# The last sum of the output done on VectorE instead of by accumulating DMAs, and layer one's last second products dealt among layer two's first products

## The chip, the cores and the metric

The kernel runs on one core of a Trainium2 chip. Time is device time in microseconds (us) of one execution; smaller is better. Engines: PE (TensorE matmul, with its weight loads PEld), DVE (VectorE), ACT (ScalarE), POOL (GpSimd), SP (SyncE, which here only issues DMAs).

## What is computed

Attention for 2 batches of 8 heads (768 tokens, head width 64) in which a query sees only the keys of its own hash bucket, then two dense layers over the 1536 tokens:

```python
attn_out = _attn_ref(**attn_kwargs)                       # masked softmax attention, f32
x = attn_out.transpose(0, 2, 1, 3).reshape(B * S, H * D)  # (1536, 512)
h = x @ w_in                                              # layer one, 512 -> 2048
g = h - np.tanh(h)
x = g @ w_out                                             # 2048 -> 512
g = x @ w_gate                                            # layer two, 512 -> 1536
silu = g * (1.0 / (1.0 + np.exp(-g)))
val = x @ w_val
out = silu * val @ w_out2                                 # 1536 -> 512
```

The weights come as 64-bit floats and are converted on the chip. Each f32 operand is split into a high and a low part, and a product is three matmul passes (high x high, high x low, low x high).

## The kernel before, in words

**Halves and blocks.** The 1536 tokens are two halves `sb` of 768 (one for each batch), and each half is two blocks `t` of 384. The hidden width is cut into chunks `i` of 256 columns: 8 for layer one, 6 for layer two.

**First products.** For a chunk and a half, `products` makes `x @ w` by Strassen's scheme: seven products `m` = 0 to 6 of six matmuls each (128x384), from seven sums of blocks of `x` (A11, S1, A12, S2, S4, S3, A22), which `x_blocks` makes ahead: ACT copies the high part (L361), DVE or POOL subtracts it for the low part (L363), and further sums come from DVE or POOL (L368). One such set of seven is a "unit". Layer one has 16 units `in`; layer two has 24, `gate` and `val` for each chunk and half. ACT and DVE take the products out of PSUM (L830, L833), form tanh or silu, and split the result for the second product (L779, L784).

**Second products.** `out_group` is one group of six matmuls into one PSUM bank (a ring of four banks). Layer one has 8 groups for each chunk and half (128x384), layer two has 6 (128x512; three, `m` = 0 to 2, for each block `t`). A group's sum is copied from PSUM by ACT or DVE (L923) to a staging slot in SBUF. When the groups of a block are staged, one DMA on POOL's queue adds the slot to what is there already: in SBUF for layer one (L931), in DRAM, to the output itself, for layer two (L940, 768 KB; the first chunk is a plain store on SP's queue, L938). Layer one's last chunk is added by DVE (L917), because the next layer's `x_blocks` reads the sum; each half's `x_blocks` is declared behind the half's last group.

**The order.** The program first lists all operations in a nominal order, with `clock` counting PE's time, and gives each a due time. `Plan.order` then plays the list: each engine takes the ready operation that is due first, with the costs written in the list; those of the second part (all behind `n_first`) are multiplied by `SAFE` except on PE. The order that it finds for each engine is the program; on the chip each engine's queue runs in that order, waiting at semaphores. The nominal order interleaves neighbouring units, and deals the second products among the first products by a `credit` for each first product: 8/7 of a group while `n` (the unit's number) is below 20, 3/7 after. When the unit that ends layer one is finished, `flush` puts out all that is left of its groups at once. What is left when the products are over follows behind them.

**Staging slots.** Layer two's four slots lie where layer one's sums were (`stage`, L749). The four (half, block) pairs take them in turn, so a chunk uses the slot that the same pair had a chunk earlier.

Of the kernel before, what the change touches and what calls it, by code (L numbers as in the profile page):

```python
# [14 lines left out]
ALU = mybir.AluOpType  # L15
# [3 lines left out]
NB, NH, S, D = 2, 8, 768, 64  # L19
NBITS = 6  # L20
NPAIR = NH // 2
TB = 384
NTK = NB * S
NSB = NTK // S
DM = 512
KT = DM // 128
F1, F2 = 2048, 1536
NP1, NP2 = F1 // 256, F2 // 256
# [36 lines left out]
class Plan:  # L65
# [4 lines left out]


    LAT = 0.14
    SAFE = 1.1

    def __init__(self):
        self.ops = []
# [3 lines left out]
    def op(self, eng, fn, r=(), w=(), due=0.0, lat=None, late=False, after=0.0, alt=None, port=()):  # L80
        n = len(self.ops)
        deps = set()
        for k in r:
            deps.update(self.writers.get(k, ()))
        for k in w:
            deps.update(self.writers.get(k, ()))
            deps.update(self.readers.get(k, ()))
        for k in r:
            self.readers.setdefault(k, []).append(n)
        for k in w:  # L90
            if k in r:
                self.writers.setdefault(k, []).append(n)
            else:
                self.writers[k] = [n]
                self.readers[k] = []
        deps.discard(n)
        eng = {e: t * (1 if e == "PE" or not self.n_first else self.SAFE) for e, t in eng.items()}
        self.ops.append((eng, fn, deps, due, self.LAT if lat is None else lat, late, after,
                         DUE["alt"] if alt is None else alt, port))
# [86 lines left out]
def lsh_attention_moe_kernel(ctx: ExitStack, tc: tile.TileContext, qT, kT, vP, proj, cst, wts, out):  # L186
# [3 lines left out]
    op = plan.op  # L190
# [48 lines left out]
    def ring(name, n):  # L239

        c = counts[name] = counts.get(name, -1) + 1
        return name, c % n
# [12 lines left out]
    def dve(n):  # L255
        return (n + 151) / 960 - 0.01
# [78 lines left out]
    def need(key, due, after=0.0):  # L335
        while key not in wkey:
            k = stream.pop(0)
            (declare_out if k[0].startswith("out") else declare_in)(*k, due, after)
        return wkey[key]
# [409 lines left out]
    def stage(layer, m):  # L749

        if m == 0:
            stages[layer] = ring(("st", layer), (2, 4)[layer - 1])[1]
        r = stages[layer]
        key = "st", layer, r, m
        size = (TB, DM)[layer - 1]
        first = []
        if key not in used:
            used.add(key)
            if layer == 1:
                first = [("xf", r, m)]  # L760
            else:
                first = [("acc", r // 2, 4 * (r % 2) + k) for k in range(m * DM // TB, ((m + 1) * DM - 1) // TB + 1)]
        if layer == 1:
            at_ = lambda n=1: ct_a[:, (8 + 4 * r + m) * TB:(8 + 4 * r + m + n) * TB]
        else:
            at_ = lambda n=1: late["acc"][r // 2][:, (r % 2) * 1536 + m * DM:(r % 2) * 1536 + (m + n) * DM]
        return at_, key, first

    stages = {}
# [3 lines left out]
        return op_t[i], k, w  # L773

    ALT = 2.0
    EARLY, XDUE, EALT, ZDUE = 14, 13, 1.0, (0, 10)

    def tt(dst, dk, a, ak, b, bk, alu, due, port):
        op({"DVE": dve(TB), "POOL": pool(TB)} if port else {"DVE": 0.56}, lambda e: e.tensor_tensor(out=dst, in0=a, in1=b, op=alu),  # L779
# [35 lines left out]
    def bank_slot():  # L815
        return RING[ring("bank", len(RING))[1]]
# [62 lines left out]
    def acc_at(sb, j, n=1):  # L879
        return late["acc"][sb][:, j * TB:(j + n) * TB]  # L880

    def out_group(layer, i, sb, j):
        d = clock[0]
        dur = 6 * (MM3, MM5)[layer - 1]
        clock[0] += dur
        name = ("out", "out2")[layer - 1]
        wks = [need((name, 2 * i + f), d) for f in range(2)]
        n = (4, 3)[layer - 1]
        t, m = divmod(j, n)
        size = (TB, DM)[layer - 1]  # L890
        gs = [gh[layer, i, sb, t, f] for f in range(2)]
        k, ps = bank_slot()
        ps = ps[:, 0:size]

        def mm(e):
            c = 0
            for f in range(2):
                w = wo_t[wks[f][1]]
                for wpart, gpart in terms:
                    if layer == 1:  # L900
                        lhs, rhs = w[:, wpart, m * 128:m * 128 + 128], gs[f][gpart]
                    else:
                        lhs, rhs = gs[f][gpart][:, m * 128:m * 128 + 128], w[:, wpart, :]
                    e.matmul(out=ps, lhsT=lhs, rhs=rhs, start=c == 0, stop=c == 5)  # L904
                    c += 1

        op({"PE": dur}, mm, r=[wk + (h,) for wk in wks for h in range(2)] + [g for gg in gs for g in gg[2]], w=[k],
           due=d, lat=0.25)
        e = clock[0]
        aks = [("acc", sb, n * t + c) for c in range(n)]  # L910
        if layer == 1 and i in (0, NP1 - 1):
            if i == 0:
                op({"DVE": dve(TB), "ACT": 0.5}, lambda g:
                   g.activation(out=acc_at(sb, j), in_=ps, func=ACTF.Copy) if g is nc.scalar else
                   g.tensor_copy(acc_at(sb, j), ps), r=[k], w=[("acc", sb, j)], due=e, late=True)
            else:
                op({"DVE": 0.57}, lambda g: g.tensor_tensor(  # L917
                    out=acc_at(sb, j), in0=ps, in1=acc_at(sb, j), op=ALU.add,
                ), r=[k, ("acc", sb, j)], w=[("acc", sb, j)], due=e, late=True)
        else:  # L920
            at_, key, first = stage(layer, m)
            op({"ACT": 0.18 + size / 1200, "DVE": dve(size)}, lambda g, at_=at_:
               g.activation(out=at_(), in_=ps, func=ACTF.Copy) if g is nc.scalar else g.tensor_copy(at_(), ps),  # L923
               r=[k], w=[key] + first, due=e, late=layer == 2, alt=EALT)
            if m == 0:
                stages[layer, "at"] = at_
            if m == n - 1:
                at_ = stages[layer, "at"]
                keys = [key[:3] + (c,) for c in range(n)]
                if layer == 1:  # L930
                    op({"POOL": 1.0}, lambda g, at_=at_: g.dma_start(out=acc_at(sb, 4 * t, 4), in_=at_(4), accum_op=ALU.add),  # L931
                       r=keys + aks, w=aks, due=e + 1, lat=5.0, late=True)
                else:
                    o = out[sb * S + t * TB:sb * S + t * TB + TB, :].rearrange("(j p) c -> p j c", p=128)
                    src = lambda at_: at_(3).rearrange("p (j c) -> p j c", j=3)
                    ok = ("o", sb, t)
                    if i == 0:
                        op({"SP": 0.5}, lambda g, at_=at_: g.dma_start(out=o, in_=src(at_)), r=keys, w=[ok], due=e + 1, lat=4.0)  # L938
                    else:
                        op({"POOL": 1.0}, lambda g, at_=at_: g.dma_start(out=o, in_=src(at_), accum_op=ALU.add),  # L940
                           r=keys + [ok], w=[ok], due=e + 1, lat=5.0)
        if layer == 1 and i == NP1 - 1 and j == 7:
            x_blocks(sb, [0, 1], lambda name, ks: acc_at(sb, ACC[name] + ks[0], len(ks)), lambda name, k: ("acc", sb, ACC[name] + k),
                     tmp_at, tmp_key, e + ZDUE[sb], True, MIX, 3)
# [19 lines left out]
    for i in range(nst):  # L964
        n, r = divmod(i, 12)
# [9 lines left out]
    units = [("in", i, sb) for i, sb in ((0, 0), (1, 0), (0, 1), (1, 1))]  # L975
# [8 lines left out]
    outs, credit, run = [], 0.0, {}  # L984
    for _, n, m in sorted(slots):
        name, i, sb = units[n]
        if m == 0:
            run[n] = products(name, i, sb)
        run[n](m)
        if m == 6:  # L990
            if name == "in":
                outs += [(1, i, sb, j) for j in range(8)]
            elif name == "val":
                outs += [(2, i, sb, j) for j in range(6)]
        credit += (8 / 7, 3 / 7)[n >= 20] if outs else 0
        flush = m == 6 and name == "in" != units[n + 1][0]
        while outs and (credit >= 1 or flush):
            credit -= 1
            out_group(*outs.pop(0))
        credit = max(credit, 0)  # L1000
    while outs:
        out_group(*outs.pop(0))
# [69 lines left out]
```

## Time and profile before

| what | before |
|---|---|
| median of 3 runs | 820.97 us (820.93 to 821.51) |
| profiled execution, its own time | 823.82 us |
| its span, first to last instruction | 822.0 us |
| PE busy | 766.3 us (93%) |
| DVE busy | 579.8 us (71%) |
| ACT busy | 470.7 us (57%) |
| POOL busy | 363.7 us (44%) |

The profiled execution took 1.8 us more than its span, and 2.9 us more than the median of the runs. Attention fills about the first 250 us of the span, layer one follows to about 516 us, layer two to the end. A busy PE is not a PE at its peak, since matmuls are pipelined and their ends are modelled.

### The profile page before, as it was taken

The numbers are of one execution on the slowest core, as the hardware profiler recorded it, in microseconds if no ns is written. First come the engines' busy times: TensorE is split into PE (matmuls) and PEld (weight loads), VectorE is DVE, ScalarE is ACT, GpSimd is POOL, SyncE is SP. The second block draws the span as 40 slices with busy tenths as digits, with TensorE's granted clock in tenths as the row PEclk, the third lists the DMA queues.
The fourth block names the chain that finished last, engine by engine and source line by source line (L and its number), as shares of the span: only waits on it lengthen the run. The fifth ranks groups of instructions, "written<-read, shape, count | busy, mean of one in ns | idle before, by whom it ended". The sixth has DMA issues, their size and how long they took to land.

```text
span 822.0 us, 12296 instructions
## 1 busy us (share of the span) xinstructions
PE 766.3 (93%) x4332; PEld 662.5 (81%) x4332; DVE 579.8 (71%) x1031; ACT 470.7 (57%) x912; POOL 363.7 (44%) x389
## 2 busy tenths in 40 slices
PE   5999999999989999999999999989999999999990
PEld 3666666666658899999999999879999999899870
DVE  6877787876798767666677678787777676777410
ACT  4787787777675655555555455645455654345430
POOL 5655566744582331554334264623353444343211
PEclk9999999999999999999999999999999999999995
DMA  8654544544122064678676725015448666765356
GB/s 212 164 133 121 121 127 113 141 107 120 40 78 77 27 154 106 145 185 191 156 167 184 162 66 128 26 66 177 142 91 179 130 143 128 151 120 95 57 86 104
DMA packets 36989, 101.09 MB, mean 123 GB/s; under 512 B 4512, under 2 KB 9888, under 8 KB 36928
## 3 DMA queue, kind: packets, MB, share of 16 engines
q1 hardware_dynamic: 24960, 64.76, 26.2%
q0 software_dynamic: 11504, 34.74, 25.1%
q10 hardware_dynamic: 464, 0.80, 0.4%
q8 instruction: 34, 0.56, 0.3%
q14 instruction: 27, 0.22, 0.1%
HBM read 46.03 MB, written 18.87 MB: 79 GB/s over the span
## 4 chain that ended last, share of the span: by engine, by line
PE 54%; DVE 8%; issue 5%; POOL 1%; ACT 1%; DMA 1%; POOLq 0%; DVEq 0%; ACTq 0%
PE s L850 25%; PE t L904 13%; PE h L904 6%; PE x L904 3%; PE x L850 3%; PE t L850 1%; DVE op L779 1%; DVE x L363 1%; DMA raw<-in_w 1%; DVE f L276 1%; PE h L850 1%; POOL out L940 1%; DVE ct L779 1%; PE x L706 1%; DVE f L279 0%
## 5 line engine op out<-in xcount | busy, mean ns | idle before, releaser
L850 PE MATMUL s<-x,wi 128*128 128x384 f32 x1200 | 235.9, 338 | 7.9 <-DVE s L779 2.1
L850 PEld LDWEIGHTS s<-x,wi 128*128 128x128 f32 x1200 | 209.7, 188 | 18.6 <-ACT op L784 3.5
L662 DVE TENSOR_REDUCE m<-s 128x1 f32<-128x768 f32 x96 | 89.4, 951 | 29.6 <-PE s L653 28.7
L671 POOL TENSOR_SCALAR ct<-ct,r 128x768 f32<-128x768 f32 x96 | 92.7, 974 | 32.9 <-DVE r L670 28.9
L664 ACT ACTIVATE ct<-s,m 128x768 f32<-128x768 f32 x96 | 85.8, 896 | 21.1 <-DVE m L662 17.1
L653 PE MATMUL s<-op 128*128 128x384 f32 x384 | 88.3, 364 | 8.8 <-ACT ct L664 8.5
L830 ACT ACTIVATE ct<-s 128x384 f32<-128x384 f32 x120 | 58.4, 491 | 64.3 <-PE s L850 63.7
L682 PEld LDWEIGHTS t<-csb,ct 128*128 128x128 f32 x576 | 64.5, 141 | 32.4 <-issue 18.9
L682 PE MATMUL t<-csb,ct 128*128 128x128 f32 x576 | 81.6, 278 | 6.3 <-POOL ct L671 2.9
L653 PEld LDWEIGHTS s<-op 128*128 128x128 f32 x384 | 65.8, 194 | 18.9 <-ACT ct L664 16.8
L904 PE MATMUL t<-op,wo 128*128 128x384 f32 x372 | 74.5, 337 | 2.4 <-DVE acc L917 1.0
L904 PE MATMUL t<-wo,op 128*128 128x512 f32 x270 | 69.1, 393 | 0.0
L706 PE MATMUL x<-pt,v 128*64 128x384 f32 x384 | 69.0, 495 | 0.0
L904 PEld LDWEIGHTS t<-op,wo 128*128 128x128 f32 x372 | 64.9, 188 | 4.9 <-ACT ct L923 1.5
L287 POOL TENSOR_TENSOR wi<-fs,wi 128x512 fp32r<-128x512 f32 (+1 forms) x39 | 59.7, 1551 | 20.3 <-ACT wi L285 19.8
L688 ACT ACTIVATE pt<-t 128x768 f32<-128x768 f32 x58 | 47.1, 812 | 29.4 <-PE t L682 28.4
L904 PEld LDWEIGHTS t<-wo,op 128*128 128x128 f32 x270 | 50.1, 188 | 8.4
L779 POOL TENSOR_TENSOR ct<-ct 128x384 f32<-128x384 f32 x24 | 24.7, 1028 | 61.8 <-ACT ct L791 30.0
L850 PE MATMUL s<-op,wi 128*128 128x384 f32 x240 | 48.6, 337 | 2.1 <-DVE ct L779 1.0
L779 POOL TENSOR_TENSOR op<-ct,op 128x384 fp32r<-128x384 f32 x24 | 24.9, 1038 | 55.4 <-ACT op L784 48.6
L940 POOL DMA_DIRECT2D out<-acc x20 | 26.2, 1310 | 49.3 <-issue 19.7
L706 PEld LDWEIGHTS x<-pt,v 128*64 128x64 f32 x384 | 24.7, 136 | 28.5 <-issue 28.5
(161 smaller groups left out, 1384.6 us busy)
## 6 DMA issues: line engine op xcount, KB each, us to landing
raw<-in_w SPq DMA_DIRECT2D x68, 512.0 KB, 3.9
acc<-ct POOLq DMA_DIRECT2D x24, 768.0 KB, 6.7
out<-acc POOLq DMA_DIRECT2D x20, 768.0 KB, 7.7
op<-raw SPq DMA_DIRECT2D x42, 192.0 KB, 3.0
op<-f SPq DMA_DIRECT2D x56, 96.0 KB, 2.5
v<-in_v SPq DMA_DIRECT2D x8, 384.0 KB, 3.1
out<-acc SPq DMA_DIRECT2D x4, 768.0 KB, 4.0
fs<-in_qT SPq DMA_DIRECT2D x7, 384.0 KB, 3.4
```

Source lines behind the costliest of these rows:

```text
L287: op({"POOL": pool(n), "DVE": dve(n)}, lambda e: e.tensor_tensor(out=lo, in0=src, in1=hi.bitcast(F32), op=ALU.subtract), r=rk + [wk + (0,) ...
L653: g.matmul(out=s[:, kh, 0:TB], lhsT=(b, a)[first][:, q0], rhs=ks[kh][0 if first else 1], start=first, stop=not first,)
L662: op({"DVE": 0.87}, lambda g: g.tensor_reduce(out=m, in_=sv, axis=AX.XY, op=ALU.max, negate=True), r=[sk + (0,), sk + (1,)], w=[mk], due=d ...
L664: op({"ACT": 0.9}, lambda g: g.activation(out=p.rearrange("p (a b) -> p a b", a=2), in_=sv, func=ACTF.Exp, bias=m, accum_out=sm), r=[sk + ...
L671: op({"POOL": 0.95}, lambda g: g.tensor_scalar(out=p, in0=p, scalar1=r, scalar2=1.0, op0=ALU.mult, op1=ALU.mult), r=[pk, rk], w=[pk], due= ...
L682: g.transpose(out=t_t[0][:, kt // 3, c0:c0 + 128], in_=p[:, kt * 128:(kt + 1) * 128], identity=ident)
L688: op({"ACT": 0.75, "DVE": 0.87}, lambda g: g.activation(out=dst, in_=src, func=ACTF.Copy) if g is nc.scalar else g.tensor_copy(dst, src), ...
L706: g.matmul(out=x[r, :], lhsT=v[:, kt, r], rhs=pt_t[ptks[e][1]][:, kt, :], start=(kt == 0), stop=(kt == NKT - 1), tile_position=(0, 64 * e),)
L779: op({"DVE": dve(TB), "POOL": pool(TB)} if port else {"DVE": 0.56}, lambda e: e.tensor_tensor(out=dst, in0=a, in1=b, op=alu), r=[ak, bk], ...
L830: op({"ACT": 0.49}, lambda e: e.activation(out=dst, in_=bank, func=ACTF.Copy), r=[bk], w=dk, due=due)
L850: e.matmul(out=bank, lhsT=w[:, wpart, wi * 256 + k * 128:wi * 256 + k * 128 + 128], rhs=x_at(sb, xn, xpart, k), start=first and m == 0, st ...
L904: e.matmul(out=ps, lhsT=lhs, rhs=rhs, start=c == 0, stop=c == 5)
```

## The change

Three things. First, the last chunk of layer two: for each of the four (half, block) pairs, a DMA on SP's queue reads the output as summed so far (five chunks) from DRAM into the pair's staging slot; then DVE adds each group's PSUM bank to its part of the slot, and a plain DMA on SP's queue stores that part (256 KB) to the output. The copy by ACT or DVE and the accumulating DMA on POOL's queue go, for this chunk alone. Second, `flush` goes: the groups that layer one has left are dealt by credit among the products of layer two's first units, at 8/7 of a group for each product as long as a group of layer one is next; groups of layer two come at 3/7 from the start, and at 6/7 in the last unit. Third, two numbers of the planner: `SAFE` from 1.1 to 1.05, and the due times of layer two's `x_blocks`, for the halves, from (0, 10) to (-4, 4).

```diff
-    SAFE = 1.1
+    SAFE = 1.05
...
-    EARLY, XDUE, EALT, ZDUE = 14, 13, 1.0, (0, 10)
+    EARLY, XDUE, EALT, ZDUE = 14, 13, 1.0, (-4, 4)
...
+        elif layer == 2 and i == NP2 - 1:
+            if m == 0:
+                parts = [stage(layer, c) for c in range(n)]
+                stages["last"] = [(at_, key) for at_, key, _ in parts]
+                o = out[sb * S + t * TB:sb * S + t * TB + TB, :].rearrange("(j p) c -> p j c", p=128)
+                op({"SP": 0.5}, lambda g, at_=parts[0][0]: g.dma_start(out=at_(3).rearrange("p (j c) -> p j c", j=3), in_=o),
+                   r=[("o", sb, t)], w=[key for _, key, _ in parts] + [k for _, _, f in parts for k in f], due=e - 25, lat=4.0)
+            at_, key = stages["last"][m]
+            op({"DVE": dve(DM)}, lambda g: g.tensor_tensor(out=at_(), in0=ps, in1=at_(), op=ALU.add), r=[k, key], w=[key], due=e)
+            op({"SP": 0.5}, lambda g: g.dma_start(out=out[sb * S + j * 128:sb * S + j * 128 + 128, :], in_=at_()), r=[key], w=[], due=e)
         else:
             at_, key, first = stage(layer, m)
...
-        credit += (8 / 7, 3 / 7)[n >= 20] if outs else 0
-        flush = m == 6 and name == "in" != units[n + 1][0]
-        while outs and (credit >= 1 or flush):
+        credit += (8 / 7 if outs[0][0] == 1 else 6 / 7 if n == len(units) - 1 else 3 / 7) if outs else 0
+        while outs and credit >= 1:
```

## Rows read from the trace of the kernel before

**Rows 1.** Busy time by stretch: PE, PEld, DVE, ACT, POOL; granted clock; DMA share, GB/s.
```profile
510.00:520.00 10.00, 10.00 (x59) 10.00 (x58) 5.81 (x12) 6.12 (x9) 8.11 (x7) 1.00 0.27 97
520.00:530.00 10.00, 8.99 (x50) 8.28 (x50) 8.60 (x15) 6.08 (x12) 6.82 (x5) 1.00 0.18 54
530.00:540.00 10.00, 8.54 (x46) 7.58 (x46) 8.24 (x14) 4.72 (x9) 1.18 (x1) 1.00 0.08 25
540.00:550.00 10.00, 8.10 (x34) 6.78 (x33) 7.60 (x15) 3.83 (x8) 3.46 (x4) 0.83 0.22 80
...
600.00:650.00 50.00, 50.00 (x264) 46.52 (x262) 37.03 (x67) 28.63 (x55) 22.11 (x20) 1.00 0.68 147
...
778.00:801.00 23.00, 21.81 (x102) 18.21 (x100) 5.66 (x11) 9.46 (x19) 5.71 (x5) 1.00 0.52 74
801.00:822.00 21.00, 0.00 (x0) 0.00 (x0) 0.00 (x0) 0.56 (x1) 2.58 (x2) 0.59 0.69 107
```

**Rows 2.** Timeline of the end: start, duration (us), engine, line, operation, count, idle before.
```profile
797.98 1.52 PE L904 MATMUL x<-wo,op 128*128 128x512 f32 x6
...
799.34 1.52 PE L904 MATMUL h<-wo,op 128*128 128x512 f32 x6
...
800.96 0.60 ACT L923 ACTIVATE acc<-h 128x512 f32<-128x512 f32 x1 [0.76 <-PE h L904]
805.48 1.29 POOL L940 DMA_DIRECT2D out<-acc  x1 [6.62 <-issue]
813.09 1.29 POOL L940 DMA_DIRECT2D out<-acc  x1 [6.33 <-issue]
```

**Rows 3.** Line 940's issues on POOL: issue to landing, all twenty.
```profile
DMA to landing us min/median/max: 7.1/7.7/9.9
```

**Rows 4.** The program's last line, POOL's queue (durations min/median/max ns, first and last start).
```profile
L1068 POOLq DRAIN  x3: 46/89/7869, 813.1 to 821.8; - x3
```

**Rows 5.** DMA issues by tile: queue, count, KB each, median us to landing.
```profile
op<-raw SPq DMA_DIRECT2D x42, 192.0 KB, 3.0
...
out<-acc SPq DMA_DIRECT2D x4, 768.0 KB, 4.0
...
op<-q SPq DMA_DIRECT2D x28, 96.0 KB, 2.2
```

**Rows 6.** Line 938's issues on SP: issue to landing, all four.
```profile
DMA to landing us min/median/max: 3.6/4.0/5.6
```

**Rows 7.** Groups by form from 550 us on: busy us, mean ns, idle before.
```profile
L923 DVE COPY acc<-t 128x512 f32<-128x512 f32 x8 | 5.5, 691 | 6.0 <-PE t L904 4.7 <-ACT wi L285 1.2
```

**Rows 8.** Line 917 on DVE (ns min/median/max, first and last start).
```profile
L917 DVE TENSOR_TENSOR acc<-t,acc x7: 540/547/556, 477.6 to 514.4; 128x384 f32<-128x384 f32 x7
```

**Rows 9.** Line 923 on DVE, the copies of layer one (same columns).
```profile
L923 DVE COPY ct<-t x18: 545/557/558, 286.5 to 492.4; 128x384 f32<-128x384 f32 x18
```

**Rows 10.** Timeline of PE between the layers.
```profile
500.55 1.20 PE L904 MATMUL h<-op,wo 128*128 128x384 f32 x6
503.23 3.41 PE L850 MATMUL s<-x,wi 128*128 128x384 f32 x18 [1.48 <-DVE s L779]
...
515.85 1.20 PE L850 MATMUL t<-x,wi 128*128 128x384 f32 x6
516.89 4.32 PE L850 MATMUL s<-x,wi 128*128 128x384 f32 x24
...
546.71 2.52 PE L904 MATMUL h<-wo,op 128*128 128x512 f32 x6
```

**Rows 11.** Timeline of DVE between the layers: the second half's last sum and last split.
```profile
516.04 0.56 DVE L917 TENSOR_TENSOR acc<-h,acc 128x384 f32<-128x384 f32 x1 [0.48 <-PE h L904]
...
539.76 0.95 DVE L363 TENSOR_TENSOR x<-acc,x 128x768 fp32r<-128x768 f32 x1
```

**Rows 12.** Timeline of SP's queue and of POOL in the last 85 us.
```profile
739.19 0.33 SPq L271 DMA_DIRECT2D raw<-in_w  x1
...
778.94 1.28 POOL L940 DMA_DIRECT2D out<-acc  x1
```

## The prediction, made before the change was run

> **What bounds the kernel now.** I read the busy time by stretch first [rows 1]. In layer two PE has no gap (50.00 of 50 us from 600 on), so there the kernel is worth what its matmuls take. Two places differ. From 801 to 822 PE does nothing: 21 us are pure tail. And from 520 to 550 PE is busy for 25.6 of 30 us while DVE is at 24.4 of 30; in the 10 us before, it was the other way round (PE 10.00, DVE 5.81).
>
> The timeline of the end says what the tail is [rows 2]. The last group's matmuls end at 800.86, and ACT starts to copy its bank at 800.96. But POOL starts its last two accumulating DMAs only at 805.48 and 813.09: they go out 7.6 us apart, with 6.3 to 6.6 us before each in which POOL waits for nothing shown ("issue"). Line 940's transfers land 7.7 us after issue [rows 3], so these go one at a time. POOL's drain behind the last one ends at 813.1 + 7.9 = 821.0 [rows 4], and the span 1.0 us later. So the tail is a queue of accumulating transfers; the sums had been staged at 801.56.
>
> The timeline of PE between the layers shows the second place [rows 10]. Three losses: 1.5 us of idle ahead of 503.23. From 515.85 to 546.71 PE does products only, 24 by the loops' order; they start 1.04 us apart where nothing holds them (515.85 to 516.89), so 25.0 of 30.9 us are work and 5.9 are lost. And the first group behind takes 2.52 us against 1.52 for its like at 799.34 [rows 2]: 1.0 more. Sum 8.4 us. A part of the last two is the clock: 0.83 granted from 540 to 550 [rows 1] means a third of these 10 us at 1.2 GHz, which costs 1.7 us, right after the gaps.
>
> **The tail.** From 800.96 to 822.0 it lasts 21.0 us now. After the change, what follows the last group is: one DVE add of a 128x512 bank, then one plain store of 256 KB. The add is not in the trace at this size; DVE's copy of such a bank takes 0.69 [rows 7], and at 384 columns add and copy cost the same (0.547 and 0.557) [rows 8, 9], so 0.69. Hand-over 0.1, as from PE to ACT (800.86 to 800.96) [rows 2]. A 256 KB store on SP isn't in the trace either: its nearest rows are 192 KB in 3.0 and 768 KB in 4.0, below them 96 KB in 2.2 [rows 5]; on the line between the first two it is 3.1, with 2.2 as one end and 5.6, the slowest of the plain 768 KB stores [rows 6], as the other. End of program 1.1 (1.0 above, 0.1 for the hand-over). 0.69 + 0.1 + 3.1 + 1.1 = 5.0 instead of 21.0: **16.0 us gained**, 13.5 to 16.9 with the ends.
>
> The Trainium skill, page "DMA: Bandwidth & Descriptors", section "Anatomy of one DMA — SWDGE (gpsimd) path", gives about 2.0 us + bytes / 436 GB/s per DMA. For 768 KB that estimates 3.8 us: the plain store's 4.0 [rows 5] agrees, the accumulating 7.7 [rows 3] is twice that. For 256 KB it estimates 2.6, by which the sum would be 0.5 us better.
>
> **What hides the other parts of it.** Eleven of the twelve adds, 7.6 us of DVE, lie beside PE: from 778 to 801 DVE is busy 5.66 of 23 us [rows 1], and a group takes PE 1.36 us (797.98 to 799.34) [rows 2], twice the add, with four banks. If that cover were gone they would cost PE 0.69 each. The copies leave ACT, four DMAs of 1.3 us leave POOL; neither bounds.
>
> The early reads must be there. The pair that is last, (1,1), has its fifth accumulation issued at 778.94 [rows 12], 21.9 us ahead of PE's end. By the new credit two more products lie behind that group (seven and twelve groups, not five and twelve), so 24.0. It lands 7.7 later, 9.9 at worst [rows 3]; the read of 768 KB takes 4.0, 5.6 at worst, by the plain stores [rows 5, 6], since a read of the output isn't in the trace: it is there 12.3 us (8.5) ahead of PE's end. Its first add is that of the third group from the end, 2.7 us ahead. Spare 9.6 us (5.8): cost 0; beyond the spare each us late is a us at the end.
>
> On SP, what is queued behind a waiting read is only other reads and the stores: the last weight load went at 739.19 [rows 12], and a chunk's four accumulations come three groups and seven products apart (3 x 1.36 + 7 x 1.04 = 11.4 us), so that the first read can't go before about 778.9 - 34 + 7.7 = 752. The stores behind (1,1)'s read wait with it and hold nothing else up. Cost 0.
>
> In the last unit twice as many groups go among the products. PE idles 1.2 us of 23 there [rows 1]; a product that waits for its bank gets a group ahead of it. I take 0.8 of it back (0 to 1.2).
>
> **Between the layers.** The eleven groups of layer one that now stand in a row or behind each other (three of chunk 6, eight of chunk 7) are dealt among the first ten products of layer two. PE's work stays the same, its order changes: DVE has little to do from 510 to 520 and too much from 520 to 550 [rows 1], since a row of bare products asks ACT and DVE for one every 1.04 us, while in the steady stretch DVE is at 74% with groups between. Eleven groups that move among the products pad 10 of the 24, which I cost in proportion to the groups: 11/24 of the 6.9 us lost behind 515.85 = **3.2 us gained**; the 1.5 ahead of it I leave. The ends: all 8.4 back, or a loss as in the first rival below.
>
> **The numbers of the planner.** A lower `SAFE` makes all later orders a little bolder. From 600 on there is no gap to win [rows 1], and a boldness that fails shows as a short wait. Nothing in the trace prices it: I take 0, and 2 us either way (an estimate: a quarter of the 8.4 that the one badly ordered stretch lost).
>
> **Sum.** 16.0 + 3.2 + 0.8 = 20.0 us. The profiled execution, 823.8 for a span of 822.0, would be 803.8 and 802.0; it was 2.9 above the median of the runs, and so I set the median at 820.97 - 20.0 = **801.0**.
>
> **Rivals.** *The second half's operands come late.* Its last sum now leaves PE with four products and six groups left that don't need it (4 x 1.04 + 6 x 1.36 = 12.3 us); before, with 12 or 13 products and six groups (21 us). Making its operands took from 516.04 to 540.71, 24.7 us [rows 11]. If it takes as long and the six groups come as late as they did, PE has 18 products' work, 18.7 us, for the 24.7 and the last two products: 24.7 + 2.1 - 18.7 = 8.1 lost instead of 3.7, and perhaps 2 us more at 1.2 GHz. For it: DVE's load. Against it: the earlier due time, and less of the first half's work left in that stretch. 801.0 + 4.4 to 6.4 = 805.4 to 807.4. The Trainium skill's page "TensorE: Matmul & The Clock Gate", Part 1, holds that PE's clock is throttled unless activity releases it. The 0.83 after the gaps agrees [rows 1]; by it this rival is the dearer the longer its gaps.
>
> *The whole stretch closes.* 5.2 us more back: 795.8. For it: DVE's total over 510 to 550 is 30.3 of 40 us, so there is room; against: the chains from product to operand stay.
>
> *The early read is late after all*: (1,1)'s accumulation slips by more than the spare; some 4 us, 805.
>
> *Slower than before: the stores go one at a time,* as POOL's transfers do [rows 2], each waiting until the one before has landed in the output. The first sum stands about 3 x 1.04 + 11 x 1.36 = 18.1 us ahead of PE's end, less 0.8 for the add: 783.6, or 779.6 with the 4.0 us gained on PE. Twelve stores 4.1 apart (the 768 KB price and a hand-over) and 1.1 end at 829.9, so a median of 828.9. It decides above (822.0 - 1.1 - 779.6) / 12 = 3.4 us a store. Against it: plain transfers on SP have their own queue, and the waits on POOL aren't said to be for a landing.
>
> **Chances.** The forecast 0.62 (its own range 797.5 to 804.5: the tail's ends, the planner's 2 us); operands late 0.21; all closed 0.09; read late 0.05; stores in a row 0.03. Leaving out the last and the outer parts of the second and third gives 796.5 to 807.0. Some 0.2% (1.6 us) is what a measurement can tell from no change: all cases but the last are faster by far more, so 0.96 faster, 0.01 the same, 0.03 slower.
>
> **What the profile after would show.** Right: no line 940 behind about 785; adds of 0.69 on DVE and stores on SP at the end, the span ending about 5 us after the last matmul; PE near 9 in 10 or more from 510 to 550, the clock at 1.00 there. Wrong: adds that wait for a DMA, stores over 3.4 us apart, PE waiting for line 363 behind the second half's last sum, or gaps where layer two ran full.

## The result, and the profile after

The changed kernel takes 803.22 us (median of 4 runs, 803.10 to 803.86) against 821.24 for the kernel before in the same comparison: a ratio of 0.9782, 95% interval 0.9765 to 0.9799. The forecast was 801.0, in a range of 796.5 to 807.0. The time is near; one of its three terms had the wrong sign, as the experiments below show. Of the four executions of e3 below, one took 2077.8 us and is left out of its figures (with it, its median is 811.9).

The end of the changed kernel, in the timeline (columns as in [rows 2]):

```profile
774.76 1.28 POOL L950 DMA_DIRECT2D out<-acc  x1 [8.08 <-PE s L850]
...
782.59 0.37 SPq L925 DMA_DIRECT2D acc<-out  x1
...
783.01 16.28 SPq L929 DMA_DIRECT2D out<-acc  x11
...
796.67 1.52 PE L904 MATMUL h<-wo,op 128*128 128x512 f32 x6
...
798.23 0.69 DVE L928 TENSOR_TENSOR acc<-h,acc 128x512 f32<-128x512 f32 x1 [0.67 <-PE h L904]
```

Against [rows 2]: the last operation that reads PSUM now starts at 798.23, and the span ends at 802.1, 3.9 us later; before, these were 800.96, 822.0 and 21.0 us. The last accumulating DMA (L950, line 940 before) goes out at 774.76. Its pair's early read (the last L925) goes at 782.59, when that transfer has landed, and eleven of the twelve stores follow. No add in the last stretch is shown to wait for a read.

The DMA issues of the changed kernel, to set beside [rows 5] (columns as there):

```profile
out<-acc POOLq DMA_DIRECT2D x16, 768.0 KB, 7.8
...
out<-acc SPq DMA_DIRECT2D x4, 768.0 KB, 4.1
acc<-out SPq DMA_DIRECT2D x4, 768.0 KB, 4.5
out<-acc SPq DMA_DIRECT2D x12, 256.0 KB, 2.0
```

Busy time by stretch (columns as in [rows 1]):

```profile
510.00:520.00 10.00, 8.88 (x52) 8.57 (x51) 8.21 (x13) 3.95 (x7) 6.99 (x6) 1.00 0.05 10
520.00:530.00 10.00, 8.57 (x48) 7.96 (x47) 5.93 (x12) 5.06 (x9) 7.15 (x5) 1.00 0.17 54
530.00:540.00 10.00, 9.35 (x48) 8.33 (x48) 9.06 (x17) 5.69 (x10) 1.28 (x1) 1.00 0.28 105
540.00:550.00 10.00, 10.00 (x55) 9.43 (x54) 8.11 (x14) 5.82 (x11) 5.61 (x5) 1.00 0.41 133
...
600.00:650.00 50.00, 48.31 (x252) 44.41 (x252) 36.37 (x66) 24.67 (x48) 24.17 (x21) 1.00 0.68 147
```

Between the layers the gaps are smaller and the clock stays at 1.00, as forecast. But from 600 to 650, where PE had no gap [rows 1], 1.7 us are idle now: one of the signs of being wrong that the prediction named. The timeline of PE shows such waits from 580 on:

```profile
583.27 1.31 PE L850 MATMUL s<-op,wi 128*128 128x384 f32 x6 [0.72 <-DVE ct L779]
588.05 2.35 PE L850 MATMUL s<-x,wi 128*128 128x384 f32 x12 [1.32 <-DVE op L779]
...
625.10 2.35 PE L850 MATMUL s<-x,wi 128*128 128x384 f32 x12 [1.47 <-DVE ct L833]
```

### The profile page after: what moved, and what is told of

It reads as the page before. It is cut to its first block, busy times and chain, and to the rows that moved or that the text cites. A ratio compares the mean times of both kernels' runs of the same rounds, so it can differ in the third digit from the quotient of the medians.

```text
span 802.1 us, 12309 instructions
## 1 busy us (share of the span) xinstructions
PE 766.6 (96%) x4332; PEld 661.5 (82%) x4332; DVE 589.4 (73%) x1038; ACT 466.8 (58%) x906; POOL 359.7 (45%) x384
## 4 chain that ended last, share of the span: by engine, by line
PE 76%; DVE 11%; DMA 4%; ACT 3%; issue 3%; POOL 2%; SPq 0%; DVEq 0%; ACTq 0%; POOLq 0%
PE s L850 26%; PE t L904 13%; PE x L706 7%; PE t L682 7%; PE s L653 7%; PE h L904 6%; PE x L904 4%; DMA raw<-in_w 3%; DVE m L662 2%; PE x L850 2%; PE t L850 1%; ACT ct L664 1%; DMA acc<-ct 1%; DVE ct L779 1%; DVE op L779 1%
## 5 line engine op out<-in xcount | busy, mean ns | idle before, releaser
L904 PE MATMUL t<-op,wo 128*128 128x384 f32 x384 | 77.0, 338 | 4.8 <-DVE acc L917 1.5
L904 PEld LDWEIGHTS t<-op,wo 128*128 128x128 f32 x384 | 66.9, 188 | 7.8 <-DVE acc L917 2.1
L287 POOL TENSOR_TENSOR wi<-fs,wi 128x512 fp32r<-128x512 f32 (+1 forms) x37 | 57.1, 1553 | 24.1 <-ACT wi L285 18.0
L324 POOL TENSOR_TENSOR wo<-f,wo 128x512 fp32r<-128x512 f32 x17 | 22.4, 1316 | 75.1 <-ACT wo L322 70.9
L285 ACT ACTIVATE wi<-fs 128x512 fp32r<-128x512 f32 (+1 forms) x60 | 41.5, 701 | 10.4 <-DVE fs L305 4.0
L779 POOL TENSOR_TENSOR ct<-ct 128x384 f32<-128x384 f32 x20 | 20.6, 1029 | 59.9 <-ACT ct L791 31.0
```

Source lines behind the costliest of these rows:

```text
L285: op({"ACT": 0.19 + n / 1175}, lambda e: e.activation(out=hi, in_=src, func=ACTF.Copy), r=rk, w=[wk + (0,)], due=due, late=late)
L287: op({"POOL": pool(n), "DVE": dve(n)}, lambda e: e.tensor_tensor(out=lo, in0=src, in1=hi.bitcast(F32), op=ALU.subtract), r=rk + [wk + (0,) ...
```

## The experiments

Theory at the start: the tail gives 16 to 17 us, the new dealing of groups between the layers gives some more, and something in the dealing takes it back behind 580 us. Rivals: the planner's numbers do what I put down to the dealing; or the tail gives less and the dealing more.

**First four: the parts one at a time.** The kernels are the changed one with parts put back. e1 and e3 have the planner's numbers of before:

```diff
-    SAFE = 1.05
+    SAFE = 1.1
...
-    EARLY, XDUE, EALT, ZDUE = 14, 13, 1.0, (-4, 4)
+    EARLY, XDUE, EALT, ZDUE = 14, 13, 1.0, (0, 10)
```

e1 and e4 have the dealing of before:

```diff
-        credit += (8 / 7 if outs[0][0] == 1 else 6 / 7 if n == len(units) - 1 else 3 / 7) if outs else 0
-        while outs and credit >= 1:
+        credit += (8 / 7, 3 / 7)[n >= 20] if outs else 0
+        flush = m == 6 and name == "in" != units[n + 1][0]
+        while outs and (credit >= 1 or flush):
```

and e2 has the tail of before:

```diff
-        elif layer == 2 and i == NP2 - 1:
+        elif False:
```

> The kernel before with the last chunk's sums on VectorE alone; SAFE, due times and dealing of groups as before, so PE's order is the one of before. Theory: the tail's 16 to 17 us are the gain of this part, whatever comes ahead of it (after the change the span ends 3.9 us behind the start of the last add, against 21.0 before): 804.0 to 805.2. Rival: the tail's transfers were partly hidden and the new dealing earns the larger part: over 808.

> The change without its tail: new dealing and new planner numbers, last chunk by accumulating DMAs as before. Theory: about 1 us from PE's order, and up to 3 more since the last unit's dealing at 6/7 lets the row of four accumulating transfers start earlier: 817 to 820.5. Rival (the other parts come to nothing): 821.

> The change with SAFE 1.1 and due times (0, 10) as before: tail and dealing alone. If the 5 us that the changed kernel loses again from 560 to 650 us come from the planner's numbers: 798 to 800. If they come from the dealing (layer two's first groups at 3/7 of a group for a product instead of 8/7): 803 to 805.

> The change with the dealing as before (8/7 below unit 20, then 3/7, rest of layer one flushed): tail and planner numbers alone. If the loss from 560 to 650 us comes from the numbers, and the gain between the layers from the dealing: 806 to 809. If both come from the dealing: 803 to 805, with PE's gaps between the layers as before.

| kernel | median us | ratio to before, 95% interval |
|---|---|---|
| e1: tail alone | 804.67 | 0.980 (0.979 to 0.981) |
| e2: all but the tail | 819.16 | 0.997 (0.996 to 0.998) |
| e3: tail and dealing | 811.11 | 0.988 (0.986 to 0.989) |
| e4: tail and planner's numbers | 802.06 | 0.976 (0.975 to 0.978) |
| all of it (the change) | 803.22 | 0.978 (0.977 to 0.980) |

The tail alone is worth 16.8 us (821.49 to 804.67), and all the rest together 1.5, with intervals that overlap. The new dealing added to the tail costs 6.4 us. The planner's numbers, which I had set at nothing, bring 2.6 with the old dealing and 7.9 with the new. My theory of the dealing falls, and the rival that the planner's numbers do it stands. The times of e3 and e4 lie outside both values that I had expected for each.

Busy time from 500 to 550, of e1, the changed kernel and e4:

```profile
500.00:550.00 50.00, 44.16 (x237) 40.64 (x236) 39.72 (x69) 24.63 (x47) 23.95 (x19) 1.00 0.29 79
...
500.00:550.00 50.00, 46.66 (x253) 43.82 (x252) 38.02 (x65) 27.93 (x52) 28.47 (x21) 1.00 0.36 98
...
500.00:550.00 50.00, 46.54 (x249) 43.21 (x248) 39.68 (x68) 28.34 (x53) 28.47 (x20) 1.00 0.30 79
```

PE is busy as long in e4, with the old dealing, as in the changed kernel: the planner's numbers alone make the gaps between the layers smaller.

Where e3 loses is seen in PE's timeline between the layers:

```profile
533.99 0.86 PE L904 MATMUL h<-wo,op 128*128 128x512 f32 x3
538.12 1.80 PE L904 MATMUL h<-wo,op 128*128 128x512 f32 x3 [3.28 <-ACT wo L322]
539.73 2.25 PE L850 MATMUL s<-op,wi 128*128 128x384 f32 x6
```

and in its busy time by stretch:

```profile
530.00:540.00 10.00, 5.21 (x19) 3.53 (x19) 9.10 (x18) 4.43 (x9) 1.23 (x1) 0.86 0.32 104
540.00:550.00 10.00, 10.00 (x43) 9.42 (x43) 6.13 (x9) 4.99 (x9) 2.18 (x3) 0.80 0.36 126
```

Halfway through a group of layer two PE waits 3.28 us for the second weight chunk. DVE, at 9.10 of 10 us, starts to convert it at 534.17, when the first chunk has left the buffer that both pass through, and makes a chunk for the first products by turns with it, until 538. During the wait or behind it the clock falls to 1.2 GHz, for 6.8 us in all (0.86 and 0.80 granted: 1.4 and 2.0 us of pulses missing at half rate), and six matmuls that take 1.2 us elsewhere take 2.25. So the clock is up to 3.4 of the 6.4 us. This is not the prediction's first rival: what is late is a weight. The second half's low parts (L363) come behind it, from 539.0 on, and no wait of PE from 500 to 560 in e3 ends with one.

In e2 the tail is as it was, four transfers one at a time. They only start earlier, at 785.05 instead of 789.81, as POOL's timeline shows; the denser dealing in the last unit and PE's being ahead of the profiled execution of before both do that:

```profile
785.05 1.30 POOL L950 DMA_DIRECT2D out<-acc  x1 [0.17 <-issue]
792.50 1.30 POOL L950 DMA_DIRECT2D out<-acc  x1 [6.15 <-ACT acc L933]
800.33 1.29 POOL L950 DMA_DIRECT2D out<-acc  x1 [6.53 <-issue]
807.70 1.28 POOL L950 DMA_DIRECT2D out<-acc  x1 [6.08 <-issue]
```

**Which number, and which half of the dealing.** e5 puts back SAFE alone, e6 the due times alone (the lines above). e7 and e8 split the dealing. In e7 layer two's groups come at 8/7 below unit 20, as before:

```diff
-        credit += (8 / 7 if outs[0][0] == 1 else 6 / 7 if n == len(units) - 1 else 3 / 7) if outs else 0
+        credit += (8 / 7 if outs[0][0] == 1 or n < 20 else 6 / 7 if n == len(units) - 1 else 3 / 7) if outs else 0
```

In e8 layer one's rest is flushed as before, and the new credits are kept:

```diff
+        flush = m == 6 and name == "in" != units[n + 1][0]
-        while outs and credit >= 1:
+        while outs and (credit >= 1 or flush):
```

> The changed kernel with SAFE 1.1 alone put back; due times (-4, 4) stay. With both numbers put back it took 811.9, with both changed 803.2. If the due times carry the difference (the second half's operands made earlier, as line 363 ends 8 to 13 us sooner where both are changed and the dealing is the old one): 803 to 805. If SAFE carries it: 810 to 812.

> The changed kernel with due times (0, 10) alone put back; SAFE 1.05 stays. If the due times carry the difference: 810 to 812, with PE's wait for prepared weights between the layers. If SAFE carries it: 803 to 805.

> The changed kernel, but below unit 20 layer two's groups are dealt at 8/7 as before instead of 3/7. If the 5 us that PE loses from 580 to 650 us come from layer two's slower start: 798 to 800, without the waits at 588 and 625 us. If they come from layer one's spread groups or from the numbers: 802.5 to 804.

> The changed kernel, but what layer one has left is flushed ahead of layer two as before; layer two's dealing as changed (3/7 from the start, 6/7 in the last unit). The kernel with all of the old dealing took 802.1. If layer one's spreading costs the 1.1 us between that one and the changed kernel: 801 to 802. If layer two's slower dealing costs it: 803 to 805.

Measured: e5 806.27 (ratio 0.979 to 0.984), e6 809.10 (0.983 to 0.987), e7 803.52 (0.975 to 0.980), e8 802.05 (0.974 to 0.978). From e3's 811.1 the due times alone take 4.8 us (e5), SAFE alone 2.0 (e6, with an interval that overlaps e3's), both 7.9: the due times do the more, and neither expectation holds alone. e6 is where the prediction's first rival is seen, PE waiting for the second half's operands:

```profile
538.93 0.44 PE L850 MATMUL s<-x,wi 128*128 128x384 f32 x1 [1.31 <-ACT x L361]
541.05 3.89 PE L850 MATMUL s<-x,wi 128*128 128x384 f32 x11 [1.68 <-DVE x L363]
```

Behind these waits the clock falls as in e3 (0.67 granted from 540 to 550); in e5 it is 1.00 from 500 to 560, so the fall may be most of the 2.8 us that e6 takes over e5.

With the new numbers, e7's faster start of layer two doesn't change the time, and e8's flush gives what e4 gave. That points to the spreading of layer one's groups as a cost of about 1.2 us (803.22 and 803.52 against 802.05 and 802.06), but the intervals overlap. By that margin e4 and e8 are ahead of the changed kernel. With the old numbers no run separates the spreading from the rest of the dealing.

How far each kernel's PE is ahead of e1's (e1 has PE's order of before), worked out from the start of every matmul in the traces: the work begun by then, counted at 1.04 us for six matmuls of 384 columns and 1.36 for six of 512.

```
at us            500    540    560    650    797
after           -0.5    0.4    3.3   -2.2    0.2
e3 tail+deal    -1.4   -4.2   -4.7   -7.4   -5.9
e4 tail+numbers  0.4    1.2    3.8    1.2    1.1
e7 two fast     -1.0   -0.3    1.5   -0.9    0.7
e8 flush kept   -1.2    0.7    2.1    0.5    1.1
```

The changed kernel is ahead by 3.3 us at 560 and behind by 2.2 at 650; with the flush kept the loss in that stretch is 1.6. In e7, which spreads layer one's groups as well, it is 2.4, but e7 had gained less by 560: the faster start of layer two changes where time is lost, and not how much. What couples the dealing to PE's waits on DVE behind 580 isn't shown: the orders on DVE and ACT differ too, and no run changes one of them alone.

**Are the second half's operands the point?** With the old dealing the new numbers make them earlier: the last low part (L363) is made by 539.8 in e1 and by 533.6 in e4. In the changed kernel it is made only by 543.1, later than in e1, and yet PE doesn't wait for it. So, on e4, earlier still: `ZDUE = (-4, -4)`.

> The changed kernel with the old dealing (as e4_tail_numbers, 802.1) and the second half's due time at -4 instead of 4. If making the second half's operands earlier is what the planner's numbers bring: 800 to 801.5. If 4 was early enough: 802 to 803.

Measured: 813.05 (0.989 to 0.992), 11 us worse than e4. The operands are there by 528.8, but the DVE made them first, and PE's timeline shows what was late in their place, a weight of layer two's first units (L287):

```profile
524.67 0.69 PE L850 MATMUL s<-x,wi 128*128 128x384 f32 x1 [3.85 <-DVE wi L287]
```

Busy time by stretch, same kernel:

```profile
520.00:530.00 10.00, 6.15 (x23) 5.83 (x22) 9.36 (x13) 5.04 (x8) 1.94 (x2) 0.66 0.10 28
```

DVE is at 9.36 of 10, and a clock of 0.66 is 6.8 us of the 10 at 1.2 GHz. "Earlier operands" is therefore not the cause of the gain by itself. As I read these runs it is a balance: between the layers operands, weights and the products' own sums pass through the same DVE, and what is put behind makes PE wait, a weight in e3 and e12, the second half's operands in e6.

**The tail by itself.** Three kernels with one edit each. In e9, on the change, the read waits for the pair's first group, and is due with it:

```diff
-                   r=[("o", sb, t)], w=[key for _, key, _ in parts] + [k for _, _, f in parts for k in f], due=e - 25, lat=4.0)
+                   r=[("o", sb, t), k], w=[key for _, key, _ in parts] + [k for _, _, f in parts for k in f], due=e, lat=4.0)
```

In e10, on the kernel before, the last chunk's transfers on POOL's queue don't add:

```diff
-                        op({"POOL": 1.0}, lambda g, at_=at_: g.dma_start(out=o, in_=src(at_), accum_op=ALU.add),
+                        kw = {} if i == NP2 - 1 else dict(accum_op=ALU.add)
+                        op({"POOL": 1.0}, lambda g, at_=at_, kw=kw: g.dma_start(out=o, in_=src(at_), **kw),
```

In e11, on the change, one store of 768 KB follows the third add:

```diff
-            op({"SP": 0.5}, lambda g: g.dma_start(out=out[sb * S + j * 128:sb * S + j * 128 + 128, :], in_=at_()), r=[key], w=[], due=e)
+            if m == n - 1:
+                at0 = stages["last"][0][0]
+                o = out[sb * S + t * TB:sb * S + t * TB + TB, :].rearrange("(j p) c -> p j c", p=128)
+                op({"SP": 0.5}, lambda g: g.dma_start(out=o, in_=at0(3).rearrange("p (j c) -> p j c", j=3)),
+                   r=[key_ for _, key_ in stages["last"]], w=[], due=e)
```

> The changed kernel, but each early read also waits for the first group of its pair, so it isn't early. A read takes 4.5 us to land in the changed kernel. Theory (the reads cost nothing because they are early): the last pair's sums stand some 4 us later, and banks are held at each of the four pairs: 807 to 815. Rival (the read is hidden by the groups anyway): 803 to 804.

> The kernel before; its last chunk's four transfers on POOL's queue overwrite the output instead of adding to it, so the addition of the first five chunks is left out. If the 21 us of tail come from accumulating (7.7 us a transfer against 4.0 for a plain one): each lands in about 4 us, the last is issued soon after the last copy, tail 7 to 9 us: 807 to 811. If POOL's queue itself takes them one at a time at 7.7 us whatever they do: 821.

> The changed kernel with one store of 768 KB for each pair behind its third add, instead of three of 256 KB. The small stores land in 2.0 us, a 768 KB store in 4.1: the end is 2.1 us later, 805.3. Rival (a store's size doesn't matter for the end, its fixed part does): 803.2.

e9: 807.39 (0.981 to 0.984), 4.2 us more. Its timeline shows the adds waiting for reads, and PE for a bank that an add holds:

```profile
791.82 0.69 DVE L928 TENSOR_TENSOR acc<-h,acc 128x512 f32<-128x512 f32 x1 [3.54 <-DMA acc<-out]
...
792.57 1.67 PE L904 MATMUL h<-wo,op 128*128 128x512 f32 x6 [1.50 <-DVE acc L928]
...
800.73 0.69 DVE L928 TENSOR_TENSOR acc<-t,acc 128x512 f32<-128x512 f32 x1 [3.02 <-DMA acc<-out]
```

So the early reads are hidden because they are early, not because groups would cover them anyway.

e10: 806.57 (0.981 to 0.985), 14.6 us less than before, with the same queue, issues and sizes, the addition alone left out. POOL's timeline, and the last stretch's issues:

```profile
796.02 0.76 POOL L941 DMA_DIRECT2D out<-acc  x1 [4.27 <-ACT acc L923]
798.74 0.77 POOL L941 DMA_DIRECT2D out<-acc  x1 [1.96 <-ACT acc L923]
```

```profile
out<-acc POOLq DMA_DIRECT2D x5, 768.0 KB, 4.0
```

The transfers are now issued when ACT has staged them, without the 6 us of waiting of [rows 2], and land in 4.0 us (the median of five, the last accumulating one among them). The old tail was the price of accumulating, not of POOL's queue. How the addition makes POOL wait isn't shown.

e11: 804.89 (0.978 to 0.982), 1.7 us more than the change; the last chunk's 768 KB stores land in 3.5 there, against 2.0 for 256 KB. Cutting the stores to 256 KB is worth the difference.

## Why the prediction was right, and where it was wrong

**The tail: right, 16.0 forecast, 16.8 measured** (e1). Of its working, the add came out as read from [rows 7] (0.69); the hand-over is 0.04 where I had 0.1. The store was mis-sized: 3.1 forecast from the line between 192 and 768 KB, 2.0 measured. That is below the 2.2 I had as the lowest end: the smaller rows were moves from one on-chip tile to another (`op<-raw`, `op<-q`) and no measure of a store to DRAM. The Trainium skill, page "DMA: Bandwidth & Descriptors", section "Anatomy of one DMA — SWDGE (gpsimd) path", would have given 2.6: nearer, still too much. It is for DMAs that GpSimd issues, and these stores are SP's. Its 3.8 for 768 KB is near the plain transfers here, on POOL (4.0, e10) and on SP (4.1, and 4.5 for the reads); the accumulating ones (7.8) it doesn't cover.

**The cover: right.** The read of (1,1) went at 782.59, and with 4.5 us to land was there at 787.1. Its first add, of the third group from the end, is the last on the bank pair `t`; the adds of line 928 (ns, first and last start):

```profile
L928 DVE TENSOR_TENSOR acc<-t,acc x6: 681/692/693, 779.3 to 796.1; 128x512 f32<-128x512 f32 x6
```

It starts at 796.1: a spare of 9.0 us, forecast 9.6 with 5.8 as the other end. e9 shows what it costs when the cover is gone.

**Stores one at a time: excluded.** From 783.01 on, eleven are issued within 16.3 us, as the groups come (1.36 us apart at the end).

**Between the layers: wrong, the step that failed.** I costed the padding of 10 of 24 products by eleven groups at 3.2 us gained, "in proportion to the groups". The new dealing costs 6.4 us by itself (e1 to e3), and about 1.2 with the new numbers (e4, e8 to the change), which is not clear of noise. The step took PE's gaps for a lack of padding alone, and looked only at how many products DVE is asked for, not at what else it has to make. In e3 the products' sums and two sets of weights meet on DVE ahead of the second half's operands: PE waits for a weight, and the clock falls. No rival of mine had that. The first one, to which I gave 0.21, is seen in e6 and not in e3; how its price came by 18 products' work isn't said, so that the price can't be worked out again. The term's sum has a slip besides: 138 matmuls start between 515.85 and 546.71, which is 23 products and not 24, so that 6.9 us were lost there and not 5.9.

**The planner's numbers: wrong.** Set at 0 with 2 us either way; they bring 2.6 us on the old dealing, and 7.9 on the new one. I had costed the due times only as a point against the first rival, though they were the one edit aimed at the resource, DVE, that I had found overloaded.

**The last unit: not separated.** 0.8 us forecast; e8 has the denser dealing there and e4 hasn't, and they take the same (802.05 and 802.06).

**The sum** came out near by luck: the two wrong terms, a loss that I had as a gain and a gain that I had as nothing, nearly cancel (4.0 forecast ahead of the tail, 1.5 measured). The gain by spans, 822.0 to 802.1, looks like the 20.0 forecast, but the timed gain is 18.0. In e1, with PE's order of before, PE's work is 2.5 us ahead of the profiled execution of before. Of these, 1.0 us is there before the stretch between the layers, and 1.5 is the clock in it: 1.00 from 500 to 550 where that execution had 0.97. So 1.5 of the 8.4 us that I counted as lost between the layers belonged to that one execution, which was 2.9 us slower than its median: I subtracted the 2.9 from the end and left the 1.5 in the term.

## What to carry to other kernels

A row of accumulating DMAs at the end of a kernel is a serial tail; reading the old sum back early, adding on a compute engine and storing plainly turns 21 us into 4, if the read has its landing time in hand. When an engine between two stages is near full, an edit that pads another engine moves the queue on it as well; ask what stands behind each item on the full engine before counting the padding as gain. And when a change has several parts, run the strongest alone: here it had all but 1.5 us of the gain, and one of the others, by itself, was a loss that a third made up.

## What the runs showed of the hardware

An accumulating DMA of 768 KB to DRAM takes 7.7 us [rows 3] where the same transfer without the addition takes 4.0, on the same queue (e10). When accumulating ones are queued up, some 6 us pass ahead of each in which POOL waits for nothing shown [rows 2]; plain ones go out when they are staged (e10).

A wait of PE of 3.3 us (e3) and one of 3.9 (e12) each came with 6.8 us at 1.2 GHz, up to 3.4 us lost beside the wait. The Trainium skill, page "TensorE: Matmul & The Clock Gate", Part 1, has PE's clock throttled unless activity releases it, and these traces agree: between the layers the clock falls only where PE has been waiting. But the waits alone don't say whether it falls. From 515 to 546 the profiled execution of before and that of e1 have the same ones, none over 1.02 us, and the clock fell in the first (0.83 from 540 to 550 [rows 1]) and not in the second (1.00). The last product ahead of the first group, before and in e1:

```profile
544.97 1.95 PE L850 MATMUL s<-x,wi 128*128 128x384 f32 x6 [0.88 <-ACT ct L798]
...
544.00 1.31 PE L850 MATMUL s<-x,wi 128*128 128x384 f32 x6 [0.87 <-ACT ct L798]
```

In the trace before, one subtraction of 128x768 on DVE (L363) took 3.23 us instead of the 0.95 of its like, beside the same operation on POOL that started 0.25 us later:

```profile
497.59 0.95 DVE L363 TENSOR_TENSOR x<-acc,x 128x768 fp32r<-128x768 f32 x1
...
498.88 3.23 DVE L363 TENSOR_TENSOR x<-acc,x 128x768 fp32r<-128x768 f32 x1
499.13 2.16 POOL L363 TENSOR_TENSOR x<-acc,x 128x768 fp32r<-128x768 f32 x1
```

e1's trace has the same pair (3.23 and 2.15). DVE's next two operations (L833, L779) end in the wait of 1.48 us that PE has ahead of 503.23 [rows 10]; in the changed kernel DVE makes these low parts without POOL, in 0.95 to 0.96 each, and PE has no such wait. There POOL is slow in its turn, 3.37 us from 498.68 on for a subtraction of weights (L287) that takes 1.80 at 744.61 before. No run here takes the two engines apart, so that one delays the other is only argued.
